# Second pass of Q and K: seven products of halves in place of four plain blocks, and the work that moves with it

## The chip, the cores and the metric

The kernel runs on one core of one Trainium2 chip. A time is device microseconds (us) of one execution. The kernel before took 1787.72 us (median of 3 executions, 1787.06 to 1787.75). The execution whose trace is read here took 1787.19 us; 1785.4 us of it is the span of the profile.

## The reference

The input x has 2048 tokens of 1024 numbers. Two branches work on it, and a gate mixes them:

```python
x = A_x
g = _sigmoid((x * gate_w).sum(-1, keepdims=True))
a = _A_ref(x, A_wqkv, A_wo)                  # 32 heads of 32; softmax(q k / sqrt(32)) v, then wo
b = _B_ref(x, B_w_q, B_k1, B_k2, B_u, B_v)   # PEER: 64 experts
return g * a + (1 - g) * b
```

In the second branch each of 32 heads multiplies x by a 1024x256 matrix `w_q`. It compares one half of the result with 8 keys `k1` and the other with 8 keys `k2`, and takes the best of each. The pair names one of 64 experts, and the output is the sum over the heads of gelu(x . u) v.

## The kernel before, in words

**Precision.** fp32 numbers are kept as a high and a low part (`split`: ACT writes the high part, DVE subtracts it to get the low one). A product of two such pairs is three matmuls per 128 rows of contraction: high by high, high by low, low by high. A 128x512 block of Q or K over the whole contraction (8 chunks of 128) is thus 24 matmuls, and a product over half the contraction is 12.

**Stages.** Q and K are made in two passes over x: tokens 1024 to 2047 first, then 0 to 1023. Each pass goes through 8 chunks of 128 output columns, for Q and K each.

- First pass: chunks 0 and 1 plain. Chunks 2 to 7 as units (`qk_unit`). A unit takes the Q and K columns of one chunk as two block rows, both halves of the contraction as two block columns, and makes the 2x2 block product with seven products of halves (`Halves`: S1 to S4 are sums of weight halves, T1 to T4 of x halves, P1 to P7 the products) in place of eight. Seven products of 12 matmuls (84) stand for four plain blocks of 24 (96).
- Second pass: all 8 chunks plain, 32 blocks of 24 matmuls (line 734).
- Router: 16 tiles of 128 tokens (`router_mm`, line 781, 24 matmuls each). DVE and POOL turn each tile into an expert number per head and side (`router_1` to `router_4`, lines 785 to 827; `router_step(t)` does the last three stages for the tiles before). The weights `Wp` of the router are `w_q` folded with the keys.
- Values: half of V plain (line 900), the rest as units (line 156). Then attention, and the output projection.

**The folds.** `w_q` times the keys is 32 `fold`s of four groups of matmuls with a 32-column stationary (line 332). Four folds share a bank; `fold_t` turns the bank round and stores the result in DRAM (WPD), from where `load_wp` fetches it and `split_wp` makes the router's weights. In the second pass a table (`between`) says after which of the 32 blocks which work is issued: nearly all folds there come in triples, behind one block.

**The evacuation.** `evac_hi` copies a result to `hi` on ACT (line 241), and `evac_lo` subtracts on DVE (line 254) and takes a largest absolute value on DVE (line 248), for a bound on the attention's scores that is compared with a limit after the router (`bound`, line 835). `store_parts` issues the two stores on ACT's DMA queue. In a unit, DVE adds the products up (line 162): P1 is copied out by ACT (line 532), then P6, P7, P5 and so on are added in SBUF.

**The gate** (z = x . gate_w) is eight multiply-adds of 128x512 on DVE for each 512 tokens (lines 663 and 665), all in the second pass; `gate_sums` adds over the partitions on PE and stores z.

**x.** The four 512-token blocks of x, in two halves each (`x_blk[n, ki]`, high and low part), stand in SBUF from the second pass to the values; those that the units have overwritten with T sums are loaded and split again in the second pass (`again`).

Each engine works through its instructions in the order in which the code issues them. In the second pass this order is set by the table; in the units by the order of the products and by the `hooks`; in the router by the loop over the tiles:

```python
for t in range(NT - 1):
    router_mm(t)
    router_step(t)
    if t >= 8 and t % 2 == 0:
        ...
        in_parts(f"B{ki + 1}{2 - ni}", ...)   # splits the V weights, 128x2048 on ACT and DVE
```

Behind the router come, on DVE, the rest of the last tiles, the experts' activation (lines 921 to 951) and, for the V units, T sums and S sums of x and weight halves with their low parts. The first V unit's products start at 509.10 us in the order P1, P2, P3, P7, ...; P1 and P2 take the weight halves in `a` (A11, A12), P3 takes the operand S4, whose low part DVE makes behind a T sum, and P7 takes S3.

## Time and profile before

| stage | us from the span's start | what PE runs |
|---|---|---|
| first chunks | 0 to 53.2 | plain blocks, tokens 1024 to 2047 |
| first pass | 53.2 to 179.8 | six units, folds 2 to 11 |
| second pass | 179.8 to 377.7 | 32 plain blocks, 20 folds |
| router | 377.7 to 465.2 | 16 tiles |
| values | 465.2 to 623 | plain, then units |
| attention | 623 to 1605 | |
| output projection | 1605 to 1785 | |

The profiled execution took 1787.19 us with a span of 1785.4 us, at a granted TensorE clock of 1.00. The median of the runs is 0.53 us above it. In the views, "busy" of PE is a modelled time of pipelined matmuls: a row of PE's timeline lasts longer than the step to the next row's start, and steps from start to start are what counts. In a DVE or ACT row, what stands in brackets is the idle time before the instruction and what ended it.

### The profile page before, as it was taken

The numbers are of one execution on the slowest core, as the hardware profiler recorded it, in microseconds if no ns is written. First come the engines' busy times: TensorE is split into PE (matmuls) and PEld (weight loads), VectorE is DVE, ScalarE is ACT, GpSimd is POOL, SyncE is SP. The second block draws the span as 40 slices with busy tenths as digits, with TensorE's granted clock in tenths as the row PEclk, the third lists the DMA queues.
The fourth block names the chain that finished last, engine by engine and source line by source line (L and its number), as shares of the span: only waits on it lengthen the run. The fifth ranks groups of instructions, "written<-read, shape, count | busy, mean of one in ns | idle before, by whom it ended". The sixth has DMA issues, their size and how long they took to land. (4 is left out here: it accounts for less than half of the span.)

```text
span 1785.4 us, 35585 instructions
## 1 busy us (share of the span) xinstructions
PE 1776.8 (100%) x14663; PEld 1006.1 (56%) x14663; DVE 1502.2 (84%) x1319; ACT 1216.6 (68%) x1613; POOL 295.8 (17%) x357
## 2 busy tenths in 40 slices
PE   9999999999999999999999999999999999999999
PEld 7777776788888843333333333333343333337887
DVE  6968776258886869999999999999999989998886
ACT  4434322221233399999999999999999999993221
POOL 0212000026501201112112121121111121221100
PEclk9999999999999999999999999999999999999999
DMA  7797888831227787779889888897898898977431
GB/s 244 240 284 246 269 276 279 280 117 72 73 100 252 272 207 164 166 162 198 186 183 210 179 194 197 179 187 169 184 205 189 182 211 191 198 160 270 140 102 72
DMA packets 138428, 343.16 MB, mean 192 GB/s; under 512 B 17452, under 2 KB 50560, under 8 KB 119940
## 3 DMA queue, kind: packets, MB, share of 16 engines
q0 software_dynamic: 24080, 139.27, 38.2%
q1 hardware_dynamic: 93876, 165.38, 28.7%
q10 hardware_dynamic: 20304, 36.18, 7.1%
q8 instruction: 116, 1.90, 0.4%
q14 instruction: 52, 0.43, 0.1%
HBM read 151.47 MB, written 86.09 MB: 133 GB/s over the span
## 5 line engine op out<-in xcount | busy, mean ns | idle before, releaser
L1154 ACT ACTIVATE P<-ring 128x512 f32<-128x512 f32 (+2 forms) x980 | 792.0, 942 | 3.2 <-PE ring L296 1.8
L1321 DVE TENSOR_TENSOR acc<-acc,P 128x2048 f32<-128x2048 f32 x199 | 455.3, 2291 | 36.9 <-ACT P L1154 23.1
L1282 PE MATMUL o<-P,V 128*32 128x512 f32 (+2 forms) x3992 | 449.3, 534 | 0.3 <-ACT P L1154 0.3
L296 PE MATMUL ring<-z,k 32*128 32x512 f32 x4224 | 345.3, 425 | 0.0
L296 PEld LDWEIGHTS ring<-z,k 32*128 32x128 f32 x4224 | 179.5, 183 | 265.0 <-ACT P L1154 200.4
L1321 DVE TENSOR_TENSOR rb<-rb,P 128x2048 f32<-128x2048 f32 x89 | 203.9, 2291 | 15.7 <-ACT P L1154 9.6
L1282 PEld LDWEIGHTS o<-P,V 128*32 128x32 f32 x3992 | 92.6, 108 | 186.3 <-issue 162.9
L296 PE MATMUL ring<-z,z 32*128 32x512 f32 x1908 | 156.5, 425 | 0.5 <-ACT P L1154 0.5
L296 PEld LDWEIGHTS ring<-z,z 32*128 32x128 f32 x1908 | 81.7, 183 | 112.8 <-ACT P L1154 76.3
L1311 POOL DMA_DIRECT2D P<-P x70 | 65.7, 939 | 374.6 <-ACT P L1154 374.6
L1154 ACT ACTIVATE wo_raw<-ring 128x512 f32<-128x512 f32 (+2 forms) x126 | 107.1, 944 | 0.0
L241 ACT ACTIVATE hi<-bk 128x512 fp32r<-128x512 f32 x40 | 23.7, 595 | 111.6 <-PE bk L734 100.0
L734 PE MATMUL bk<-xh,e 128*128 128x512 f32 x384 | 94.2, 394 | 0.0
L734 PE MATMUL bk<-xl,e 128*128 128x512 f32 x384 | 92.3, 389 | 0.0
L734 PEld LDWEIGHTS bk<-xh,e 128*128 128x128 f32 x384 | 71.0, 188 | 22.0 <-issue 3.4
L254 DVE TENSOR_TENSOR lo<-bk,hi 128x512 fp32r<-128x512 f32 x40 | 27.5, 688 | 65.2 <-ACT hi L241 65.2
L734 PEld LDWEIGHTS bk<-xl,e 128*128 128x128 f32 x384 | 72.1, 188 | 15.0
L1321 DVE TENSOR_TENSOR acc<-acc,wo_raw 128x2048 f32<-128x2048 f32 x32 | 73.3, 2292 | 4.6 <-ACT wo_raw L1154 1.4
L1154 ACT ACTIVATE vhl<-ring 128x512 f32<-128x512 f32 (+2 forms) x90 | 76.2, 923 | 0.0
L102 DVE TENSOR_TENSOR e<-wraw,e 128x512 fp32r<-128x512 f32 (+3 forms) x64 | 54.4, 857 | 25.3 <-ACT e L101 24.7
L156 PE MATMUL pa<-woh,acc 128*128 128x512 f32 x224 | 72.5, 389 | 0.0
L1329 POOL DMA_DIRECT2D acc<-acc x41 | 32.8, 800 | 229.2 <-DVE acc L1321 123.4
(304 smaller groups left out, 2484.7 us busy)
## 6 DMA issues: line engine op xcount, KB each, us to landing
P<-P POOLq DMA_DIRECT2D x70, 1024.0 KB, 10.0
wqt<-in_wq SPq DMA_DIRECT2D x26, 1024.0 KB, 6.7
wraw<-in_wqkv SPq DMA_DIRECT2D x30, 512.0 KB, 7.9
acc<-acc POOLq DMA_DIRECT2D x21, 512.0 KB, 8.4
qdh<-hi ACTq DMA_DIRECT2D x32, 256.0 KB, 5.5
qdl<-lo ACTq DMA_DIRECT2D x32, 256.0 KB, 6.0
kdh<-hi ACTq DMA_DIRECT2D x32, 256.0 KB, 2.6
kdl<-lo ACTq DMA_DIRECT2D x32, 256.0 KB, 5.7
```

The lines of the kernel that those rows point to most:

```text
L102: (on or nc.vector).tensor_tensor(out=lo, in0=src, in1=hi.bitcast(F32), op=OP.subtract)
L156: nc.tensor.matmul(ps, self.a[a][i][:, k, :], self.b[b][j][k], start=(not first and k == 0 and i == j == 0), stop=(k == HC - 1 and i == 1))
L241: nc.scalar.activation(hi, src, AF.Copy)
L254: nc.vector.tensor_tensor(out=lo, in0=src, in1=hi.bitcast(F32), op=OP.subtract)
L296: yield j, nc.tensor.matmul(ps, a[rows], b[rows], start=(i == 0), stop=(i == 2))
L734: nc.tensor.matmul(ps, t[:, kc // HC, a, kc % HC], x_at(b, n, kc), start=first, stop=last)
L1154: return nc.scalar.activation(to, ps, AF.Exp, scale=SCALE, bias=-SHIFT_LIMIT)
L1282: nc.tensor.matmul(O[h][32 * j:32 * j + 32, c0:c1], Vt[g][:, kt, 32 * j:32 * j + 32], p[:, j * 512 + c0:j * 512 + c1], start=(kt == 0), st ...
L1311: nc.gpsimd.dma_start(P[h, b], P[h, a], accum_op=OP.add)
L1321: nc.vector.tensor_add(out, a, b)
L1329: nc.gpsimd.dma_start(ACC[h][:n], ACC[h][n:2 * n], accum_op=OP.add)
```

## The change

What it does, part by part:

1. **Second pass by units.** Chunks 0 and 1 stay plain (8 blocks by `plain_block`), chunks 2 to 7 become six units. `qk_unit` serves both passes (`NB` is the first block of tokens). The T sums for it are made during the plain blocks, in places of x blocks.
2. **Three products add onto P1's bank.** In both passes P6, P7 and P4 are accumulated on P1's PSUM bank (`onto`). ACT copies the bank to SBUF after P1, after P6 and after P7; DVE adds P2 to the first copy, P5 and P3 to the second, P5 to the third. What stands in the bank after P4 is evacuated as it is. The order of the products is P1, P5, P6, P2, P7, P3, P4 (in the unit of chunk 2: P1, P2, P6, P3, P7, P5, P4).
3. **Operand copies.** The S sums move from POOL to DVE, and the copies to high and low parts follow tables (`PARTS`, `PARTS2`).
4. **Bound.** The largest absolute value on DVE becomes a sum of squares by ACT (`Square` with `accum_out`) into `junk`; the limit is squared, and what is compared is a product of two sums.
5. **Folds singly**, one between two products, in both passes (`fold_at`).
6. **The gate** is made in pieces of two multiply-adds between products, in `z`, stored in DRAM (ZPD). Parts of two token blocks (8 multiply-adds) move to the router, and `gate_sums` behind the router's tile 10.
7. **Router weights** go into the places of the units' operands; seven of the eight chunks are split in the last unit, the last one right behind it.
8. **x blocks** (1,0), (2,1), (2,0), (3,0) and (3,1) are loaded and split again during the router, at tiles 0, 2, 3, 5 and 6 (`more_x`); the first two loads (1 MB each) are issued by `load_spare` in the last unit of the second pass.

```diff
-        def product(self, name, first=None, bank=None):
+        def product(self, name, first=None, bank=None, onto=None):
             a, b = self.FACTORS[name]
-            ps = (bank or self.bank)()
+            ps = onto or (bank or self.bank)()
...
-                                     start=(not first and k == 0 and i == j == 0),
+                                     start=(not first and not onto and k == 0 and i == j == 0),
...
         nc.scalar.activation(hi, src, AF.Copy)
+        nc.scalar.activation(junk, src, AF.Square, accum_out=sq4[:, which, c, n:n + 1])
...
-        maxima.append((amax4[:, which, c, n:n + 1], hi.bitcast(F32)))
...
+        for name in order:
+            if name in ("P6", "P7", "P4"):
+                p[name] = hq.product(name, onto=p["P1"])
+            else:
+                p[name] = hq.product(name)
+            if name in ("P1", "P6", "P7"):
+                u[name] = cp.tile([128, 512], F32, name=f"u{name}")
+                nc.scalar.activation(u[name], p[name], AF.Copy)
+            made = parts.get(name, ()) if nxt else ()
+            for a in made:
+                hq.hi(a)
...
+            if name == "P1" and late:
+                evac_lo()
+            if name == "P2":
+                tt(u["P1"], u["P1"], p["P2"])
+                out(0, nb, u["P1"])
...
+            if name == "P4":
+                out(1, nb, p["P4"])
+            for a in made:
+                if a != "A11":
+                    hq.lo(a)
+                if a == "S3":
+                    hq.sums("S2")
+                    hq.sums("S4")
...
+            for f, *args in hooks.get(name, ()):
+                f(*args)
             store_parts()
...
+    ORDER = "P1", "P5", "P6", "P2", "P7", "P3", "P4"
+    PARTS = dict(P1=("A11",), P5=("S1",), P2=("A12",), P7=("S3",), P3=("S2",), P4=("S4", "A22"))
...
+    plain_block(1, 1, 1, [(hq.parts, "A22"), (hq.parts, "S1"), (combine, "T4", "xh1"), (load_w, 1, 3)])
...
+    hooks[7]["P1"] += [(wr.close,), (open_router,)]
+    hooks[7]["P6"] += [(split_wp, 0), (split_wp, 1), (split_wp, 2), (load_spare,)]
+    hooks[7]["P2"] += [(split_wp, 3)]
+    hooks[7]["P7"] += [(split_wp, 4)]
+    hooks[7]["P3"] += [(split_wp, 5), (split_wp, 6)]
+    for c in range(2, KC):
+        qk_unit(c, ORDER2 if c == 2 else ORDER, c + 1 if c < KC - 1 else None, hooks[c])
+    evac_lo()
+    store_parts()
+    nc.vector.tensor_reduce(sq, sq4, axis=AX.X, op=OP.max)
...
+    split_wp(7)
...
+    load_xr(2, 0, 0)
+    load_xr(3, 0, 1)
+    gate_load(1)
+    more_x = {0: [(from_spare, 1, 0, "xh1"), (lambda: gate(0, xr[1, 0]),)], 2: [(from_spare, 2, 1, "xl3"), (gate_store, 1)],
+              3: [(from_spare, 2, 0, "xh2"), (load_xr, 3, 1, 0), (gate_load, 3)],
+              5: [(from_spare, 3, 0, "xh3"), (lambda: gate(0, xr[3, 0]),)], 6: [(from_spare, 3, 1, "xl2")],
+              7: [(gate_store, 3), (load_zacc,)], 10: [(gate_sums,)]}
     for t in range(NT - 1):
         router_mm(t)
         router_step(t)
+        for f, *args in more_x.get(t, ()):
+            f(*args)
```

How the order of instructions moves is seen at three places. First PE in the second pass. In a row, the first name is the tile written, the names behind the arrow are the tiles read (`bk` a PSUM bank, `e` a weight operand, `xh`/`xl` a place of x, `wqt` a place of `w_q`), and the number at the end counts equal rows. Before, three folds stand in one stretch between two blocks:

```order
L734 MATMUL bk_2691<-xl_1468,e_141 128x512 x12
L332 MATMUL bk_2599<-wqt,kpad 32x512 x4
L332 MATMUL bk_2599<-wqt_1591,kpad 32x512 x4
L332 MATMUL bk_2599<-wqt_1592,kpad 32x512 x4
L734 MATMUL bk_2741<-xh_1523,e_141 128x512 x12
L734 MATMUL bk_2741<-xl_1547,e_141 128x512 x12
L353 MATMUL bk_2773<-ident,wt 128x128 x4
```

Now, in the unit of chunk 6, the products P1, P5, P6, P2, P7, P3, P4 with a fold after P5, P2 and P3; P6, P7 and P4 write the bank of P1:

```order
L167 MATMUL bk_2634<-xh_1474,e_143 128x512 x12
L167 MATMUL bk_2656<-xl_1668,e_144 128x512 x12
L338 MATMUL bk_2593<-xh_1964,kpad 32x512 x4
L167 MATMUL bk_2634<-xl_1753,e_144 128x512 x12
L167 MATMUL bk_2692<-xl_1545,e_154 128x512 x12
L338 MATMUL bk_2593<-wqt,kpad 32x512 x4
L167 MATMUL bk_2634<-xh_1706,e_143 128x512 x12
L167 MATMUL bk_2743<-xl_1569,e_154 128x512 x12
L338 MATMUL bk_2593<-xh_1964,kpad 32x512 x4
L167 MATMUL bk_2634<-xh_1924,e_154 128x512 x12
```

What moved: each fold has a product on either side, and the last product of a unit ends in a bank that started with its first. Second, DVE at the router's first tiles. Before (`router_1` of one tile, then `router_2`):

```order
L789 TENSOR_REDUCE m<-bk_3011 128x64
L790 TENSOR_SCALAR m<-m 128x64
L792 TENSOR_TENSOR eq<-bk_3011,m 128x64x7
L794 TENSOR_SCALAR eq<-m 128x64
L802 TENSOR_REDUCE mm<-eq 128x64
L804 TENSOR_TENSOR eq<-eq,mm 128x512
```

Now, with what each instruction waits for (15 more memsets of one column stand behind the first row; Activation, DVE and Pool are the engines ACT, DVE and POOL, and DMAHW0 to DMAHW7 the lanes on which the hardware DMA queues report their transfers):

```order
L767 MEMSET e_3008 128x1 [waits DMAHW4_49,DMAHW3_49]
L812 TENSOR_REDUCE m<-bk_3033 128x64 [waits DMAHW6_49,Activation_49]
L813 TENSOR_SCALAR m<-m 128x64 [waits DVE_49]
L815 TENSOR_TENSOR eq<-bk_3033,m 128x64x7 [waits DMAHW5_49,DVE_49]
L817 TENSOR_SCALAR eq<-m 128x64
L173 TENSOR_TENSOR xh_3066<-xh_2886,xh_3066 128x2048 [waits Activation_49]
L617 SCALAR_TENSOR_TENSOR junk<-xh_2886,gw,junk 128x512 [waits DMAHW6_49]
L617 SCALAR_TENSOR_TENSOR junk<-xh_2886,gw,junk 128x512 [waits DVE_49] x3
L825 TENSOR_REDUCE mm<-eq 128x64 [waits DMAHW7_49,Pool_49]
L827 TENSOR_TENSOR eq<-eq,mm 128x512 [waits DVE_49]
```

What moved: between `router_1` of tile 0 and the next tile stand the low part of an x block (128x2048) and four gate operations, and the first rows wait for transfers. Third, ACT at the end of the last unit of the second pass, now (before, ACT went from the last stores of a plain block to splitting the last two router weights, and then to `xu`):

```order
L254 ACTIVATE hi<-bk_2795 128x512 [waits DMAHW4_49,PE_49]
L255 ACTIVATE junk,sq_138<-bk_2795 128x512 [waits Activation_49]
L85 DMA qdh<-hi 128x512 [waits DMAHW1_49]
L85 DMA qdl<-lo 128x512 [waits DMAHW2_49,DVE_49]
L85 DMA kdh<-hi 128x512 [waits DMAHW3_49,Activation_49]
L85 DMA kdl<-lo 128x512 [waits DMAHW5_49,DVE_49]
L103 ACTIVATE e_154<-wpr_2884 128x448
L103 ACTIVATE e_154<-ugr 128x64
L808 ACTIVATE xu<-bk_3033 128x64 [waits DMAHW3_49,DMAHW6_49,DMAHW1_49,PE_49]
```

What moved: the split of the last router weight (into the place `e_154`) stands behind four stores, and the stores of `qdl` and `kdh` wait on lanes 2 and 3, whose transfers before these are the two 1 MB loads of `load_spare`.

## The prediction

> **What bounds the kernel now.** I read the page's busy shares first, then the busy time by stage, then the timelines of PE and DVE where stages meet, and last the groups that give prices.

> ```profile
> PE 1776.8 (100%) x14663; PEld 1006.1 (56%) x14663; DVE 1502.2 (84%) x1319; ACT 1216.6 (68%) x1613; POOL 295.8 (17%) x357
> core 0: us, PE busy (x) PEld busy (x) DVE busy (x) ACT busy (x) POOL busy (x), PEclk, DMA share, GB/s
> 53.20:179.80 126.60, 126.39 (x600) 97.62 (x597) 97.82 (x128) 47.72 (x77) 30.43 (x23) 1.00 0.82 259
> 179.80:377.70 197.90, 197.90 (x957) 149.96 (x956) 118.55 (x163) 53.72 (x77) 3.84 (x5) 1.00 0.83 264
> 382.75:429.94 47.19, 47.19 (x210) 38.80 (x209) 32.94 (x66) 3.93 (x10) 25.30 (x31) 1.00 0.26 91
> 429.94:465.00 35.06, 35.06 (x157) 29.02 (x156) 32.36 (x52) 6.87 (x9) 23.11 (x24) 1.00 0.00 0
> 465.00:514.01 49.01, 49.01 (x217) 40.28 (x216) 44.57 (x55) 15.13 (x18) 10.79 (x12) 1.00 0.22 76
> ```

> PE alone sets the time up to the values: it stands still for 0.2 us in the first pass and never after it. But the reserve behind it differs. In both passes DVE has a quarter or more of the time free. In the first half of the router it is idle for 47.19 - 32.94 = 14.25 us; from 429.94 us on it is nearly dense (32.36 of 35.06, then 44.57 of 49.01). Work that goes to DVE in the router has only those 14 us to go into. The next rows show what is waited for behind it:

> ```profile
> 500.41 1.29 DVE L102 TENSOR_TENSOR a<-xw,a 128x512 fp32r<-128x512 f32 x2
> 513.33 0.68 DVE L102 TENSOR_TENSOR xh<-xw,xh 128x512 fp32r<-128x512 f32 x1
> 516.14 1.28 DVE L102 TENSOR_TENSOR xh<-z,xh 128x512 fp32r<-128x512 f32 x2
> ...
> 509.10 2.91 PE L156 MATMUL bk<-xh,a 128*128 128x512 f32 x12
> 514.60 2.88 PE L156 MATMUL bk<-xl,xh 128*128 128x512 f32 x12
> ```

> The first V unit takes S4 at 514.60 us, which DVE has ready at 513.33 + 0.68 = 514.01: 0.59 us of reserve. Its A parts are ready at 501.70 for a product at 509.10: 7.4 us. So DVE's queue is a second path, nearly as long as PE's at 514 us, that starts with the router.

> **Part 1, fewer products.** A product of halves steps by 2.72 us, 0.2267 per matmul:

> ```profile
> 190.72 2.88 PE L734 MATMUL bk<-xh,e 128*128 128x512 f32 x12
> 193.44 2.88 PE L734 MATMUL bk<-xl,e 128*128 128x512 f32 x12
> ```

> Six units of 84 for 24 blocks of 24 matmuls take 72 away: **-16.3 us**. The first pass keeps its 84 per unit.

> **Part 2, single folds.**

> ```profile
> 198.88 2.88 PE L734 MATMUL bk<-xl,e 128*128 128x512 f32 x12
> 205.54 2.66 PE L734 MATMUL bk<-xl,e 128*128 128x512 f32 x11
> 265.01 2.88 PE L734 MATMUL bk<-xl,e 128*128 128x512 f32 x12
> 273.40 2.89 PE L734 MATMUL bk<-xl,e 128*128 128x512 f32 x12
> 306.86 1.07 PE L680 MATMUL bk<-zacc,ones 128*32 128x512 f32 x8
> 307.74 2.76 PE L332 MATMUL bk<-wqt,kpad 128*32 128x512 f32 x24
> ```

> Between 198.88 and 205.54 lie two products and one fold: 6.66 - 5.44 = 1.22 us for it. Between 265.01 and 273.40 lie two products and three folds: 8.39 - 5.44 = 2.95. A join that is cut costs (3 x 1.22 - 2.95) / 2 = 0.355. Eight triples and a pair are cut, 17 joins: **+6.0**. The sums of the gate leave this stage: **-0.9** (306.86 to 307.74). The passes lose 11.2 us.

> **Part 3, what the units ask of DVE and ACT.**

> ```profile
> L162 DVE TENSOR_TENSOR u<-u,bk 128x512 f32<-128x512 f32 x24 | 16.0, 682 | 0.3
> L102 DVE TENSOR_TENSOR e<-wraw,e 128x512 fp32r<-128x512 f32 x35 | 28.3, 815 | 11.0 <-ACT e L101 10.6
> L101 ACT ACTIVATE e<-wraw 128x512 fp32r<-128x512 f32 x34 | 20.8, 621 | 11.6 <-DVE wraw L138 5.7 <-POOL wraw L138 3.8 <-DVE lo L254 2.1
> L532 ACT ACTIVATE c<-bk 128x512 f32<-128x512 f32 x6 | 3.5, 580 | 0.0
> ...
> L665 DVE SCALAR_TENSOR_TENSOR zacc<-xh,ugr,zacc 128x512 f32<-128x512 f32 x22 | 16.5, 750 | 0.6
> L241 ACT ACTIVATE hi<-bk 128x512 fp32r<-128x512 f32 x31 | 18.5, 597 | 106.0 <-PE bk L734 96.8 <-issue 3.5 <-DVE amax L248 3.4
> L101 ACT ACTIVATE e<-wraw 128x1024 fp32r<-128x1024 f32 x15 | 15.9, 1057 | 19.1 <-DMA wraw<-in_wqkv 10.6 <-DVE zacc L665 7.4 <-ACT hi L241 1.0
> ```

> A unit with three folds takes PE 84 x 0.2267 + 3 x 1.22 = 22.7 us. DVE has four adds, four low parts of results and four S sums at 0.68, seven low parts of weights at 0.82 and some six gate operations at 0.75: 18.4 us. ACT has three copies at 0.58, four results at 0.60, seven weight parts at 0.62, and four Squares. No row has a Square that sums; I bound it by 0.597 (the same shape) and 1.057 (twice the width) and take the lower end, whose shape it has: 10.9 us, 12.7 at the upper end. Neither engine reaches PE's 22.7. P6, P7 and P4 must wait until ACT has copied P1's bank, but one whole product (2.72 us) of another bank lies before each of the three, against a copy of 0.58; the cover goes only where ACT's queue is over 2 us late. I take +0.7 over all twelve units for such meetings, between 0 and 4 (a copy's 0.58 in six of them). The sums that leave POOL, the maxima that leave DVE and the adds saved lie in DVE's and POOL's free time: nothing.

> **Part 4, the router.** DVE now also splits five x halves there and runs eight gate operations.

> ```profile
> 383.65 0.62 DVE L789 TENSOR_REDUCE m<-bk 128x64 f32<-128x448 f32 x1 [0.91 <-ACT xu L785]
> 429.94 2.78 DVE L102 TENSOR_TENSOR xh<-xh,xh 128x2048 fp32r<-128x2048 f32 x1 [0.74 <-ACT xh L101]
> 453.31 2.28 DVE L102 TENSOR_TENSOR xh<-xh,xh 128x2048 fp32r<-128x2048 f32 x1
> 455.51 0.68 DVE L827 TENSOR_REDUCE packed<-pq 128x16 f32<-128x512 f32 x1
> 460.08 0.68 DVE L827 TENSOR_REDUCE packed<-pq 128x16 f32<-128x512 f32 x1
> ...
> 377.76 0.39 PE L781 MATMUL bk<-wph,xh 128*128 128x512 f32 x1
> ```

> A low half costs 455.51 - 453.31 = 2.20, a gate operation 0.75: 5 x 2.20 + 8 x 0.75 + 0.4 for two small operations of the new bound = 17.4 us. A router step that follows such work takes 460.08 - 455.51 = 4.57. I count from PE's first router matmul (377.76). Before, the first reduction starts at 5.9 and tile 8's first stage ends at 429.20 (429.94 less the wait), that is 51.4. Now it ends at 5.9 + 1.5 (tile 0) + 8 x 4.57 + 17.4 = 61.4. DVE is 10.0 us late there; the wait of 0.74 and the slower operation (2.78 for 2.28) at 429.94 are swallowed, and 8.7 stay, since behind it DVE is dense.

> Then the start. What the first reductions wait for now are the last stores of the results: before, ACT had issued the last one by 379.81, 2.0 us after the router's first matmul. Now P3's result comes just ahead of P4's, and a high part, a Square and two stores (0.6 + 0.6 + 0.8) more stand in the queue: 4.0 us.

> ```profile
> 379.39 0.42 ACTq L83 DMA_DIRECT2D kdl<-lo  x1
> kdh<-hi ACTq DMA_DIRECT2D x32, 256.0 KB, 2.6
> kdl<-lo ACTq DMA_DIRECT2D x32, 256.0 KB, 5.7
> xl<-in_xT SPq DMA_DIRECT2D x3, 1024.0 KB, 12.6
> ```

> Landing takes 2.6 to 5.7 us, so DVE's first row is free at about 6.6 to 9.7 where it started at 5.9: +0.7 to +3.8, I take +2.2, the middle.

> S4 is then ready at 136.25 + 8.7 + 2.2 = 147.15 after the router's first matmul, and P3 took it at 136.84: **+10.3** (the 0.9 of the gate's sums, now in the router, goes into that wait). The A parts are ready at 123.94 + 10.9 = 134.8, where PE is at 132.2; so PE waits twice, 2.6 us at P1 and 147.15 - 140.3 = 6.9 us at P3. Behind the waiting P3 stands everything up to the last V unit, and behind that the attention, which ACT fills; nothing makes the loss good.

> **The clock.** The kernel has one long stretch without PE, its end:

> ```profile
> 1782.00:1783.00 1.00, 0.00 (x0) 0.00 (x0) 0.32 (x1) 0.00 (x0) 0.00 (x0) 1.00 0.12 44
> 1783.00:1784.00 1.00, 0.00 (x0) 0.00 (x0) 0.00 (x0) 0.00 (x0) 0.00 (x0) 0.87 0.63 218
> 1784.00:1785.40 1.40, 0.00 (x0) 0.00 (x0) 0.00 (x0) 0.00 (x0) 0.00 (x0) 0.50 0.00 0
> ```

> After more than 1.7 us without a matmul the granted clock is 0.50. A wait of 6.9 us should do the same, and P3 would run at half speed. How soon the clock comes back no row shows. The cost lies between 0 and 2.6 (P3 wholly at half speed is 5.44, and P7 would have waited for S3 anyway, ready 2.81 after S4 by the DVE rows at 513.33 and 516.14). I take **+2.0**, nearer the upper end, as the wait is long against 1.7. [...]

> **Sum:** -16.3 + 6.0 - 0.9 + 0.7 + 10.3 + 2.0 = +1.8 against the profiled 1787.19, thus 1789.0; the median of the runs lies 0.5 above the profiled one: **1789.5 us**.

> **Rivals.**

> *The gain arrives.* DVE makes up for most of its extra work: its waits for ACT's `xu` and for POOL vanish when it is late, and the x splits move into them more than my steps of 4.57 allow. If 3 of the 8.7 us are left and the stores land early, PE waits 3 us or less, and the clock stays: 1787.7 - 10.5 + 3 = 1780.2; with 6 left, 1783.2. For it speaks the idle 14.25 us, nearly as much as the added 17.4; against it that I have already used up 7.4 of it, and that a step seen behind other work still takes 4.57. Between: 1782.

> *The stores come late (slower).* In the last unit, `load_spare` puts two 1 MB loads on lanes that the stores of `qdl` and `kdh` must wait for. Such a load landed in 12.6 us; they are issued after the third of seven products, some 11 us before the router, and share the engines with each other. If they land at 12.6, the stores go out as I assumed; if they take twice that, 25 us, ACT's queue stands until 14 us after the router's start, with the router's last weight and `xu` behind the stores, and DVE starts some 6 us later than assumed. Beyond 2 us it decides: 1789.5 + 5 = 1794.5. For it speaks the DMA share of 0.83 in the second pass; against it that the loads of weights have ended by then.

> *The units stall.* Each unit waits 0.6 us or so at three copies for ACT: 12 x 0.6 = 7, thus 1796. Against it stands ACT's load of about half.

> *The change does not do what it says*, because the new bound sends the kernel the general way: only if the drawn inputs exceed the limit, which they do not by a wide margin (largest product of sums 12,879, worked out from the inputs, against 28,800).

> **How the numbers follow.** The forecast's own case gets 0.45, the gain 0.29, the late stores 0.20, the stalls 0.05, the last 0.01. In the likeliest case the bounds (start 0.7 to 3.8, meetings 0 to 4, clock 0 to 2.6) give 1785 to 1794. With the two neighbours the range is 1781 to 1795. About 0.2% (3.6 us) is what a measurement tells from no change, so "same" is 1784.2 to 1791.3: faster 0.30 (the gain), same 0.41 (the forecast without its upper tail), slower 0.29 (late stores, stalls, that tail).

> **What would show it.** In the profile after: the router's first matmul 10 to 11 us earlier (367) with PE dense before it; DVE's first router reduction 6.6 to 9.7 after that; DVE without waits for `xu` after tile 0; tile 8's first stage ending near 63.6 after the router's start; a PE wait of some 7 us at the first V unit's P3, with a lower clock behind it. The forecast is wrong if DVE reaches S4 less than 5 us late, if ACT's stores are issued later than 7 us into the router, or if the units lose more than 4 us.

## The result: 3% slower, most of it in the first pass

The changed kernel took 1840.66 us (median of 4, 1838.66 to 1844.44) beside 1787.39 before: a ratio of 1.0302 (95% interval 1.0282 to 1.0321). The prediction was 1789.5 with a range to 1795. The profiled execution took 1838.66 us with a span of 1836.9, 51.5 more than before. By stages, read from PE's timeline:

| stage | before | after | difference | predicted |
|---|---|---|---|---|
| up to the first unit | 53.2 | 54.3 | +1.0 | 0 |
| first pass, six units | 126.6 | 160.0 | +33.4 | +4.6 |
| second pass | 197.9 | 194.8 | -3.1 | -15.1 |
| router's first matmul to the first V unit | 131.3 | 149.7 | +18.3 | +12.3 |
| behind it | 1276.3 | 1278.1 | +1.8 | 0 |

(The two predicted figures of the passes are the prediction's sum of -10.5, split by where the folds stand: two folds more and three cut triples in the first pass, 2 x 1.22 + 6 x 0.355 = 4.6. Differences are taken before rounding.)

The page's busy row, and the stages (busy time of PE, its weight loads, DVE, ACT and POOL; then the granted clock, the share of the DMA engines and GB/s):

```profile
PE 1783.9 (97%) x14591; PEld 999.0 (54%) x14591; DVE 1524.8 (83%) x1352; ACT 1293.8 (70%) x1812; POOL 277.5 (15%) x337
54.26:214.28 160.02, 141.31 (x617) 102.91 (x614) 97.08 (x140) 70.94 (x140) 2.43 (x3) 0.93 0.77 232
214.28:409.12 194.84, 185.12 (x862) 134.76 (x861) 123.97 (x172) 92.00 (x187) 3.75 (x5) 0.99 0.79 242
422.00:470.00 48.00, 48.00 (x214) 39.39 (x213) 43.85 (x81) 13.20 (x16) 25.81 (x23) 1.00 0.41 142
501.36:558.79 57.43, 46.12 (x194) 37.68 (x193) 52.08 (x70) 12.03 (x15) 19.86 (x22) 0.88 0.19 65
```

PE, which before stood still for 0.2 us in the first pass, now stands still there for 18.7 and runs at 0.93 of its clock, while DVE, at 97 of 160 us, is no busier than it was. No engine is full: somebody waits in a queue. PE's list of waits (engine, line and what it waited for; us in total, times, longest), and PE's timeline with the five waits of the first pass:

```profile
PE bk L167 <- DVE lo L261: 20.4, 6, 6.4
PE bk L954 <- DMA zt<-zd: 11.3, 1, 11.3
PE bk L167 <- ACT uP L545: 5.7, 2, 2.9
```

```profile
62.82 4.31 PE L167 MATMUL bk<-xh,e 128*128 128x512 f32 x12 [2.82 <-ACT uP L545]
94.37 7.33 PE L167 MATMUL bk<-xl,e 128*128 128x512 f32 x24 [2.92 <-ACT uP L545]
117.38 4.27 PE L167 MATMUL bk<-xl,e 128*128 128x512 f32 x12 [1.86 <-DVE lo L261]
147.14 5.49 PE L167 MATMUL bk<-xl,e 128*128 128x512 f32 x12 [4.73 <-DVE lo L261]
179.18 5.10 PE L167 MATMUL bk<-xl,e 128*128 128x512 f32 x12 [6.38 <-DVE lo L261]
```

After each wait the product itself is longer than its 2.88 us (7.33 for 5.74 where the row holds two products): over the five rows the granted clock was 0.66, 0.77, 0.67, 0.50 and 0.56. The queues of DVE and ACT before the longest of these waits show why:

```profile
167.32 0.69 DVE L152 TENSOR_TENSOR e<-wraw,e 128x512 fp32r<-128x512 f32 x1 [2.74 <-ACT e L148]
177.11 0.69 DVE L142 TENSOR_TENSOR wraw<-wraw,wraw 128x512 f32<-128x512 f32 x1 [9.09 <-DMA wraw<-in_wqkv]
177.83 0.69 DVE L142 TENSOR_TENSOR wraw<-wraw 128x512 f32<-128x512 f32 x1
178.44 0.68 DVE L261 TENSOR_TENSOR lo<-bk,hi 128x512 fp32r<-128x512 f32 x1
...
179.16 0.34 ACTq L85 DMA_DIRECT2D kdl<-lo  x1
179.60 0.63 ACT L148 ACTIVATE e<-wraw 128x512 fp32r<-128x512 f32 x1 [12.31 <-DVE lo L261]
180.61 0.59 ACT L545 ACTIVATE uP<-bk 128x512 f32<-128x512 f32 x1
```

At the head of a unit DVE subtracts S3, which needs K's weights for the next chunk. They are still being loaded: DVE stands for 9.09 us. Behind S3 on DVE is the low part of the last unit's last result (line 261), made straight from the bank in which P4 ended, and P2 of the new unit takes that bank next; ACT's queue holds the store of the low part, and behind the store the copy of P6 that P7 needs. It starts at 180.61, though P6 had begun at 169.78 and takes 3.0 us: ACT had stood for 12.31 us. So one late transfer stops DVE, ACT and PE.

The weights were just as late before: in the units, S3 was begun 10.6 to 16.4 us after the unit's first product, and is now begun after 9.5 to 14.0 (the first products counted out in steps of 2.72 us). In the old trace it was POOL that made S3 (its waits in the first pass, and its timeline), and nothing stood behind it on POOL that made PE wait. (Of the 98.0 us, 65.7 are POOL's first wait, which began before the units.)

```profile
POOL s L138 <- DMA wraw<-in_wqkv: 98.0, 4, 65.7
```

```profile
83.57 1.29 POOL L138 TENSOR_TENSOR s<-wraw,wraw 128x512 f32<-128x512 f32 x1 [9.08 <-DMA wraw<-in_wqkv]
108.56 1.29 POOL L138 TENSOR_TENSOR s<-wraw,wraw 128x512 f32<-128x512 f32 x1 [11.60 <-DMA wraw<-in_wqkv]
133.59 1.28 POOL L138 TENSOR_TENSOR s<-wraw,wraw 128x512 f32<-128x512 f32 x1 [11.62 <-DMA wraw<-in_wqkv]
```

The timelines of PE, DVE and SP's queue at the router and the values:

```profile
409.12 0.84 PE L804 MATMUL bk<-wp,xh 128*128 128x512 f32 x3
416.75 1.38 PE L804 MATMUL bk<-e,xl 128*128 128x512 f32 x3 [2.71 <-ACT e L103]
423.22 0.06 DVE L767 MEMSET e<- 128x1 f32 x1 [5.87 <-DMA kdh<-hi]
423.58 0.62 DVE L812 TENSOR_REDUCE m<-bk 128x64 f32<-128x448 f32 x1
480.05 0.22 DVE L817 TENSOR_SCALAR eq<-m 128x64 f32<-128x64 f32 x1
...
522.02 0.31 SPq L85 DMA_DIRECT2D zt<-zd  x1
523.70 0.26 PE L954 MATMUL bk<-ident,zt 16*128 16x16 f32 x1 [11.31 <-DMA zt<-zd]
523.89 13.31 PE L937 MATMUL bk<-xl,xl 128*128 128x512 f32 x48
558.79 1.54 PE L167 MATMUL bk<-xh,a 128*128 128x512 f32 x6
```

DVE's first reduction comes 14.5 us after the router's first matmul (5.9 before), tile 8's first stage ends at 71.2 (51.4 before). The last store was issued at 415.59, 6.5 us after the router's first matmul. PE waits 11.31 us, not at P1 and P3 as predicted but earlier, at the transposition of z, and the block behind it takes 13.31 us for 11.04, at a granted clock of 0.83.

### The profile page after: what moved, and what is told of

Read it like the earlier page. It is cut to its first block, busy times and chain, and to the rows that moved or that the text cites. A ratio compares the mean times of both kernels' runs of the same rounds, so it can differ in the third digit from the quotient of the medians.

```text
span 1836.9 us, 35630 instructions
## 1 busy us (share of the span) xinstructions
PE 1783.9 (97%) x14591; PEld 999.0 (54%) x14591; DVE 1524.8 (83%) x1352; ACT 1293.8 (70%) x1812; POOL 277.5 (15%) x337
## 5 line engine op out<-in xcount | busy, mean ns | idle before, releaser
L167 PE MATMUL bk<-xl,e 128*128 128x512 f32 x504 | 131.2, 415 | 23.4 <-DVE lo L261 20.4
L167 PEld LDWEIGHTS bk<-xl,e 128*128 128x128 f32 x504 | 99.6, 201 | 55.1 <-DVE lo L261 23.0
L167 PE MATMUL bk<-xh,e 128*128 128x512 f32 x504 | 123.0, 398 | 2.8 <-ACT uP L545 2.8
L167 PEld LDWEIGHTS bk<-xh,e 128*128 128x128 f32 x504 | 93.7, 189 | 37.4 <-issue 7.5
L148 ACT ACTIVATE e<-wraw 128x512 fp32r<-128x512 f32 x70 | 42.9, 627 | 98.4 <-DVE lo L261 62.1
L152 DVE TENSOR_TENSOR e<-wraw,e 128x512 fp32r<-128x512 f32 x70 | 47.4, 687 | 41.0 <-ACT e L148 38.0
L85 POOL DMA_DIRECT2D wpd<-wt x8 | 6.2, 773 | 387.3 <-ACT wt L362 387.3
## 6 DMA issues: line engine op xcount, KB each, us to landing
P<-P POOLq DMA_DIRECT2D x70, 1024.0 KB, 10.8
wqt<-in_wq SPq DMA_DIRECT2D x17, 1024.0 KB, 8.1
xh<-in_wq SPq DMA_DIRECT2D x9, 1024.0 KB, 10.5
qdh<-hi ACTq DMA_DIRECT2D x32, 256.0 KB, 3.9
qdl<-lo ACTq DMA_DIRECT2D x32, 256.0 KB, 3.5
kdh<-hi ACTq DMA_DIRECT2D x32, 256.0 KB, 5.8
```

The source lines that it names most:

```text
L85: return queue.dma_start(a, b)
L148: nc.scalar.activation(self.a[name][0], self.raw[name], AF.Copy)
L152: nc.vector.tensor_tensor(out=lo, in0=self.raw[name], in1=hi.bitcast(F32), op=OP.subtract)
L167: nc.tensor.matmul(ps, self.a[a][i][:, k, :], self.b[b][j][k], start=(not first and not onto and k == 0 and i == j == 0), stop=(k == HC - ...
```

## The experiments

In what follows "router" is the time of the router's first matmul (377.76 before, 409.12 after, 367 by count without a wait), and "to V" is the time from there to the first V unit's first product (131.3 and 149.7). The kernel before, run beside them, took 1787 to 1790; the runs were made in batches, and totals of different batches can differ by these 2 to 3 us. Each is a single run unless a range is given. How much chance is in one trace is seen where nothing was changed: kernels with the same passes differ by up to 3.5 us in the router's start (374.81 and 378.28 below), kernels with the same router by up to 1.5 us in to V (149.5 to 151.0). Theory A is that the order of DVE's and ACT's queues makes the loss in the units, its rivals that the weights are late for any order (B) or the transfer engines full (C). Theory E is that DVE's queue from the router's start sets where the V units begin.

**The low part first.** In `qk_unit`:

```diff
+            if name == "P1" and late:
+                evac_lo()
             made = parts.get(name, ()) if nxt else ()
             for a in made:
                 hq.hi(a)
...
-            if name == "P1" and late:
-                evac_lo()
```

> One line moved in the units of both passes: the low part of the unit's last result (DVE) is issued ahead of the next operand's copies and sums, not behind them. Theory A (queue order): PE waits because that low part, and with it ACT's store and its copies, stands on DVE behind S3, which waits for K's weights. Then the waits of PE for DVE's low part (20.4 us, 6 times) go to about 0; what is left is ACT's copy of P6 behind the high part of S1, which still waits for the weights: up to 4 us per late load, some 10 us in all, with the router's first matmul at 375 to 385 us in place of 409.12. Theory B (late weights stall PE whatever stands behind them): the waits only change their name, router's start at 400 or later. In both, the wait for zt in the values stays at 11 us.

**Four buffers** for the raw weights:

```diff
-        i = w_no[0] % 3
+        i = w_no[0] % 4
...
-        nc.scalar.activation(junk, src, AF.Square, accum_out=sq4[:, which, c, n:n + 1])
+        nc.scalar.activation(lo, src, AF.Square, accum_out=sq4[:, which, c, n:n + 1])
```

> Four buffers for the raw weights in place of three (the Square writes into the low part's tile, which frees the room), order of instructions as in the change. K's weights for the next chunk but one no longer wait for the last unit's operands. Theory A and B both say that the weights' lateness goes: DVE's waits for them (26.3 and 19.6 us in the two passes) fall to below 5 us, and the router's first matmul comes at 368 to 374 us (367 is the count without any wait). If the loads are late because the transfer engines are full (theory C), the waits stay above 15 us in each pass and the router's start above 395.

Both edits together:

> Both edits. Theory A: no wait in the units is left, router's start at 367 to 371 us, little better than four buffers alone; theory C: like the low part first alone. The router and the values are untouched: DVE's first reduction some 14 us after the router's start, the wait for zt about 11 us, total about 1800 us.

| | total | router | PE's waits in the units |
|---|---|---|---|
| low part first | 1818.38 | 388.02 | copies on ACT 9.2 us, fold turn 3.1 |
| four buffers | 1814.93 | 384.45 | one for the low part 6.2, copies 4.8 |
| both | 1813.68 | 383.28 | copies 4.7, fold turn 3.6 |

Each edit alone brings the router 21 and 25 us forward, both 26. Low part first leaves the weights as late as they were (DVE still waits 21.9 and 25.4 us for them in the two passes) and still regains 21.1: it is the order, as theory A says. Theory B falls with that, and theory C with the second edit, which cuts DVE's waits for weights to 9.7 and 2.5 us. But the forecasts were too good (375 to 385, found 388; 368 to 374, found 384), and with both edits 16 us above the count are left where at most 4 were expected.

**The sums on POOL again**, the changed kernel otherwise:

```diff
-                    hq.sums("S3")
-                    hq.sums("S1")
+                    hq.sums("S3", nc.gpsimd)
+                    hq.sums("S1", nc.gpsimd)
```

> The changed kernel with one part of the change undone: the sums S3 and S1, which wait for K's weights at the head of a unit, are made on POOL again, not on DVE; the order of everything else and the three buffers stay. Theory A (DVE's queue held by the weights): DVE no longer waits for weights (26.3 and 19.6 us before), the low part of the last result goes out in time, and the waits of PE for it (20.4 us) vanish; the high part of S1 on ACT still waits, so the units keep some waits for ACT's copy of P6; router's first matmul at 380 to 392 us in place of 409.12. Theory B (the weights come too late for any order): 400 or later.

Router at 400.38, total 1830.91: 8.7 us regained, less than theory A said, and just past the line that was drawn for theory B (400 or later). The waits for the low part are gone, but

```profile
PE bk L167 <- ACT uP L545: 16.4, 7, 3.8
ACT e L148 <- POOL wraw L142: 42.3, 4, 12.1
```

(PE's waits, and ACT's in the first pass): now ACT's queue is held: the high part of S1 waits for POOL's sum, and behind it stands the copy of P6, for which P7 waits since it adds onto the same bank. That is the second half of the theory, and the next run takes it alone.

**S1 behind the copy of P6** (three buffers, low part first):

```diff
-    PARTS = dict(P1=("A11",), P5=("S1",), P2=("A12",), P7=("S3",), P3=("S2",), P4=("S4", "A22"))
+    PARTS = dict(P1=("A11",), P6=("S1",), P2=("A12",), P7=("S3",), P3=("S2",), P4=("S4", "A22"))
```

> Three buffers, low part first as in that run (router's first matmul 388.0 us there), and one thing more: ACT makes the high part of S1, which waits for K's weights, behind its copy of P6, not ahead of it (S1 moves from P5 to P6 in the table of operands). Theory A, second half (what the weights' lateness still cost after the first edit went through ACT's queue): PE's waits for ACT's copies (9.2 us, 5 times) fall to about 4 (the unit of chunk 2 keeps its 2.8), the wait for the turn of the folds (3.1) goes, router at 378 to 382. If the weights themselves are too late by now, it stays at 386 or more.

PE's waits in this kernel:

```profile
PE bk L954 <- DMA zt<-zd: 9.3, 1, 9.3
PE bk L167 <- ACT uP L545: 6.3, 4, 2.6
PE bk L804 <- ACT e L103: 4.6, 1, 4.6
```

Router at 373.93, better than forecast, total 1805.16; the fold's turn is no longer waited for. Two changes of order, with the weights little earlier than they were (DVE still waits 23.3 and 18.8 us for them, 26.3 and 19.6 in the changed kernel), move the router by 35.2 us: the passes are now 3.8 us faster than in the kernel before.

**The folds in triples again** (on both first edits): all three folds of a unit at P3.

```diff
-        fold_at(n, 3 + i // 3, ("P5", "P2", "P3")[i % 3], n + 3 if n < 9 else None,
+        fold_at(n, 3 + i // 3, "P3", n + 3 if n < 9 else None,
```

(and likewise in the second pass.)

> On top of low part first and four buffers: seven groups of three single folds (2 to 10 in the first pass, 20 to 31 but for two in the second) stand together behind P3 again. By the price of the prediction (1.22 a single fold, 2.95 a triple) the router's first matmul comes 7 x 0.71 = 5.0 us earlier, at 378.3 in place of 383.3. If single folds cost nothing more here, or if PE then waits for copies whose cover the folds were, it stays at 382 to 385.

The router comes at 392.40, 9.1 us later (total 1822.82), not 5.0 earlier. The single fold's price is what the prediction said: from 382.92 to 392.31 us in the changed kernel lie three products and one fold, 9.39 - 3 x 2.72 = 1.23. But what the folds do for the queues is worth more: PE's waits for ACT's copies grow from 4.7 us (2 times) to 12.3 (9 times), for the fold's turn from 3.6 to 7.5, and DVE's wait for weights from 9.6 to 17.0 in the first pass and from 3.8 to 11.6 in the second. A single fold lies between two products as cover, and its 1 MB load is issued alone. Which of the two counts more was not separated.

**The router's loads.** First the two loads of the last unit are issued behind the last stores:

```diff
-    hooks[7]["P6"] += [(split_wp, 0), (split_wp, 1), (split_wp, 2), (load_spare,)]
+    hooks[7]["P6"] += [(split_wp, 0), (split_wp, 1), (split_wp, 2)]
...
     evac_lo()
     store_parts()
+    load_spare()
```

> The two 1 MB loads of x for the router are issued behind the last stores of Q and K, not in the middle of the last unit. Theory D (the stores wait behind these loads): ACT issues the last store about 3 us after the router's first matmul in place of 6.5, DVE's first reduction comes 7 to 9 us after it in place of 14.5, PE's wait for the router's last weight (2.71) goes, and the wait for zt falls from 11.3 to about 5, unless the x blocks that now land later hold DVE up at tiles 0 and 2. Total 6 to 9 us less than 1838.7. Rival: the first rows of DVE wait for landings that take as long without the loads; then the start stays above 12 us. The units are untouched (router's start at 409).

Total 1843.39. DVE's first reduction comes 15.2 us after the router's first matmul (428.83 after 413.60), not 7 to 9. But the edit did not do what it was meant to do. The queues of SP and ACT, in the changed kernel (first row) and in this one:

```profile
402.03 0.97 SPq L85 DMA_DIRECT2D xh<-in_xT  x2
406.51 0.97 SPq L85 DMA_DIRECT2D xh<-in_xT  x2
420.90 0.34 ACTq L85 DMA_DIRECT2D kdh<-hi  x1
421.77 0.58 ACT L103 ACTIVATE e<-wpr 128x448 fp32r<-128x448 f32 x1 [3.40 <-DMA xh<-in_xT]
```

SP issues the two loads 7.1 us before the router's first matmul in both kernels: moving the lines of code does not hold SP back, whose queue comes to these loads behind the fetches of the router's weights either way. And the store of `kdh` goes out 7.3 us into the router, behind a stand of ACT that the profile puts down to one of these loads. So theory D, by which the stores wait for the lanes of these two loads, was not tested, and stays open. Next the other two loads of the router's start go to ACT's queue behind tile 0 (on both unit edits):

```diff
-    load_xr(2, 0, 0)
-    load_xr(3, 0, 1)
...
-    more_x = {0: [(from_spare, 1, 0, "xh1"), ...
+    more_x = {0: [(load_xr, 2, 0, 0, nc.scalar), (load_xr, 3, 0, 1, nc.scalar), (from_spare, 1, 0, "xh1"), ...
```

> On top of both edits of the units (low part first, four buffers): the two 1 MB loads of x that the router's start issues go to ACT's queue behind tile 0's work, so that only the two loads of the last unit and the stores are under way at the router's start. Theory D2 (the last stores land late because 4 MB of loads share the engines with them, not because of the lane order): DVE's first reduction comes 8 to 11 us after the router's first matmul in place of 14.9, PE's wait for the last router weight shrinks from 3.6 to below 2, and the wait for zt from 9.4 to about 5; first V product 143 to 146 us after the router's first matmul in place of 149.5. Rival (the order of ACT's queue alone: buffers and lanes): nothing changes, the start stays at 14 us or more. If the later x blocks become the limit, DVE waits at tiles 3 and 5.

The first reduction comes at 10.5 us (394.25 after 383.77) for 14.9, DVE's wait for the store of `kdh` shrinks from 5.45 to 1.65, and to V is 146.1 for 149.5; PE's waits shrink less than forecast (the last router weight 3.6 to 2.9, zt 9.4 to 7.3). The total is 1809.19 for 1813.68, but the kernel before, too, was 2.1 us faster beside this run. ACT issues the last store hardly earlier (6.6 us into the router, 7.1 without the edit); the stores land earlier. So some 4.4 of the 8.6 us that DVE starts late come from these two loads standing where they did. That they slow the stores by sharing the transfer engines is the author's guess (in the changed kernel the DMA share was 1.06 from 409.30 to 416.00 us), but it is not shown alone: the 256 KB load of z, which had stood behind them on SP's queue, goes out with the edit at 377.70 in place of 390.05.

**DVE's work in the router** (each on both unit edits, to V 149.5 there; the times from the router's first matmul decide, since the totals come from two batches). Without the gate:

```diff
-(from_spare, 1, 0, "xh1"), (lambda: gate(0, xr[1, 0]),)]
+(from_spare, 1, 0, "xh1")]
```

(the same at tile 5)

> On top of the same two edits, the eight gate operations in the router are left out (the gate's sums of these tokens are then incomplete); the loads and stores around them stay. Theory E (DVE's queue through the router sets the end of the wait for zt, one for one): 8 x 0.75 to 0.9 = 6 to 7 us of DVE work go, the wait for zt falls from 9.4 to about 3, the first V product comes 143 us after the router's first matmul in place of 149.5. Rival F (zt waits for the chain of gate stores, loads and sums): the wait falls only if that chain shortens, by 2 us or less.

Without the low parts of the remade x:

```diff
     def from_spare(n, ki, place):
-        again(n, ki, place, xr[n, ki])
+        again_hi(n, ki, place, xr[n, ki])
+        no_low.add((n, ki))
```

> On top of the same two edits, the low parts of the five x blocks that are remade in the router are left out (the matmuls read the high part in their place). Theory E: 5 x 2.2 to 2.5 = 11 to 12 us of DVE work go, more than the wait for zt, which vanishes; the first V product comes about 140 us after the router's first matmul, and the clock stays at 1.00 in the values. Rival F: the wait for zt stays near 9.

And a place for zt that does not wait for the router's end:

```diff
-    zt = sm2.tile([NT, 128], F32, name="zt")
+    zt = sm.tile([NT, 128], F32, name="zt")     # beside packed, ahead of the router
```

> On top of the same two edits, the tile zt gets a place of its own in the router's first pool, so that its load need not wait until the router's last tiles leave theirs. Theory E (DVE is late as a whole): PE no longer waits at zt, but at the first V unit's products instead, for the A parts at P1 or S4 at P3, together 6 to 10 us; the total changes by less than 3 us. Rival G (only zt's place makes the loss): the wait goes and comes back nowhere, total 9 to 11 us less than 1813.7.

| | total | to V | PE waits in the values for |
|---|---|---|---|
| both unit edits | 1813.68 | 149.5 | zt 9.4 us |
| without gate | 1807.93 | 143.9 | zt 3.4 |
| without low parts | 1801.82 | 139.3 | S4's parts at P3 0.9 |
| zt early | 1813.01 | 149.4 | the gate's bank 6.8, P3 0.7 |

Theory E holds: taking 6 to 7 us of DVE work away takes 5.6 us off, taking 12 away takes 10.2 off and the wait for zt with it. Giving zt a place moves the wait to the next thing that hangs on DVE, not to P1 or P3 as forecast, and leaves to V as it was: PE waits for ACT's copy of the gate, and ACT's row ahead of it had stood 26.5 us until a T sum of DVE's was done. Where PE waits is chance; that DVE is late is the cause.

**Repairs together.** Five more kernels combine them. The first has both unit edits, triples, the loads on ACT's queue, and T4's parts behind the copy of P1 in the unit of chunk 2:

```diff
-             [..., (hq.parts, "S1"), (combine, "T4", "xh3"), (folds, (1,), (2,))]]
+             [..., (hq.parts, "S1"), (folds, (1,), (2,))]]
...
-    hooks[2]["P1"] += [(to_spare, "xl3"), (load_wq, 3), (load_wq, 4)]
+    hooks[2]["P1"] += [(combine, "T4", "xh3"), (to_spare, "xl3"), (load_wq, 3), (load_wq, 4)]
```

(and likewise in the second pass.)

> Low part first, four buffers, folds in triples, the router's first x loads behind ACT's queue, and T4's parts behind the copy of P1 in the unit of chunk 2 (its wait of 3.0 us at P6 and the slow clock behind it go). By the sum of the parts: 1813.7 - 5 (folds) - 4.5 (loads, as measured) - 4 (T4) = 1800; DVE's lateness in the router (17 us of low parts and gate operations) stays, so it does not beat the kernel before (about 1788).

1818.2 us (median of 4, 1815.1 to 1821.3; ratio 1.0172, 1.0155 to 1.0189), 18 more than forecast. The router comes at 391.60, as late as with the triples alone (392.40), and PE's waits for copies (11.2 us) and for the fold's turn (6.7) are like those of the triples. With single folds, S1 at P6 (the edit above) and T4 moved in the first pass alone:

> Low part first, four buffers, S1 at P6, T4's parts behind the copy of P1 in the first pass, the router's first x loads on ACT's queue, single folds. Both queues repaired and the weights early: no wait in the units but small ones, the count without waits is 367; router's first matmul at 370 to 375, the router and values as with the loads on ACT's queue alone (first V product 146 us later), total 1795 to 1801.

1800.93 us, router at 374.81, to V 146.7: the fastest of the runs with the change, and at the upper end of what was forecast. Then the experts' activation in pieces, behind P1, P2, P3, P7 and P4 of the first V unit and P7, P5, P6 and P2 of the second:

```diff
-    peer_counts()
...
-    Ahl = peer_act(ng)
...
+            for f in PEER.get((u, k), ()):
+                f()
```

> As the one before, and the experts' activation (about 13 us on DVE that stood ahead of the first V unit's operands) is cut into pieces that are issued within the first two V units. Theory E (DVE's queue from the router to the first V unit is the second path): what PE waits for at the first V unit then comes from DVE 13 us earlier; the wait for zt (7 us) stays, since it hangs on the router's last tile, so the total gains less than 3 us and may lose where the pieces stand ahead of the next unit's operands.

1813.64: to V is 145.6, which is no difference beside the scatter, but PE then waits 8.65 us for the activation at its transposes behind the second V unit. Another 3.5 us are the router's start (378.28), ahead of which nothing was changed. Then the gate out of the router as well, made from the raw x in a plain block of each pass:

```diff
+              (folds, (0,), (1,)), (lambda: gate(0, raws[0][:, :, 512:], True),), (gate_store, 3)],
...
+                          (lambda: gate(0, raw_of(1, 0), True),)])
```

> As the one before, and the gate of the two token blocks is made in the two passes from the raw x (4 and 8 operations; the router has none). Theory E: 6 to 7 us of DVE work leave the router and the wait for zt goes; first V product 139 to 141 us after the router's first matmul; total 7 us less than the one before, about 1790, unless DVE in the passes has no room for the 12 operations (9 us in 100 us with 80% load).

1808.69 (median of 4; ratio 1.0123, 1.0106 to 1.0140), 5 less than the one before, not 7, and not about 1790: to V falls to 136.2 and the wait for zt to 0.9, as theory E says; the other wait, 8.66, stays. (In this kernel the gate reads places of x that the sums T had overwritten already, so its z holds other sums than the reference's; the amount of work is the same.) The last two, without and with the activation in pieces, make the gate before the T sums (four operations ahead of the first pass's units, eight at the end of its last unit), and split the last router weight ahead of the last stores:

```diff
+    gate(0, raws[0][:, :, 512:], True)
+    gate_store(3)
     for name, place in (("T1", "xh0"), ("T3", "xl1")):
...
-    hooks[7]["P4"] += [(lambda: again_lo(1, 1, raw_of(1, 1)),)]
+    hooks[7]["P4"] += [(lambda: again_lo(1, 1, raw_of(1, 1)),), (lambda: gate(0, raw_of(1, 0), True),),
+                       (lambda: gate(1, raw_of(1, 1)),), (gate_store, 1)]
...
+    split_wp(7)
     evac_lo()
     store_parts()
...
-    split_wp(7)
```

> All repairs of the units (low part first, four buffers, S1 at P6, T4 behind the copy of P1), the router's first x loads on ACT's queue, no gate operation in the router (they are made in the passes from the raw x before the T sums overwrite it), and the last router weight split ahead of the last stores. Theory E: the router starts at 373 to 379 us, PE does not wait for the last router weight, the wait for zt is below 1 us, the first V product comes 135 to 138 us after the router's first matmul (131.3 in the kernel before), total 1787 to 1794: level with the kernel before or a little slower, since the five low parts stay in the router.

> The same, with the experts' activation cut into pieces within the first two V units and its transposes one unit later (after the third). If DVE's queue up to S4 is still what PE waits for, the first V unit starts or runs 2 to 4 us earlier than in the one before; if that wait is gone already, the pieces only load the V units, and the total is the same or up to 4 us worse.

1804.47 (median of 4; 1.0092, 1.0075 to 1.0108) and 1807.53 (median of 4; 1.0112, 1.0095 to 1.0129), where 1787 to 1794 was forecast. To V is 139.0 and 135.8, so the router is near the kernel before, but it starts at 385.5, not at 373 to 379: the passes had no room for the gate at those places. Waits in PE's timeline of the first of the two, and below them SP's queue there:

```profile
44.51 3.29 PE L535 MATMUL bk<-xh,e 128*128 128x512 f32 x12 [1.78 <-ACT e L103]
169.25 12.80 PE L167 MATMUL bk<-xh,e 128*128 128x512 f32 x48 [2.54 <-ACT uP L566]
215.15 1.94 PE L337 MATMUL bk<-wqt,kpad 128*32 128x512 f32 x8 [3.46 <-DMA wqt<-in_wq]
278.52 4.50 PE L167 MATMUL bk<-xl,e 128*128 128x512 f32 x12 [2.60 <-ACT uP L566]
...
186.20 22.50 SPq L85 DMA_DIRECT2D zpd<-z  x2
208.80 0.37 SPq L85 DMA_DIRECT2D wqt<-in_wq  x1
```

The longest of them is the same mistake in a third queue. The store of the eight new gate operations holds SP's queue for 11.0 us until DVE has done them, and the load of `wqt` behind it goes out at 208.80, where it went out at 197.47 in the kernel of 1800.93 us.

No version beat the kernel before. What stays open is whether the gate can be placed in the passes without these waits.

## Why the prediction was wrong, step by step

- **Part 1 and 2, counts: right.** A product steps by 2.72 us and a single fold costs 1.23. But the 6.0 us called a loss was no loss that could be undone: triples cost 9.1 more.
- **Part 3, what the units ask of DVE and ACT, is the step that failed.** It said that the sums which leave POOL "lie in DVE's and POOL's free time: nothing". Their working time does; their waiting does not. POOL waited 9 to 12 us for the weights in each of three units of the old trace, and the change moved that wait, with the sums, into the queue of an engine that others wait for. The prediction counted busy time (18.4 and 10.9 of 22.7 us) and took that for room (in the first pass DVE's free time was 23%, a little less than the quarter that it read). It is only half of it, though: with the sums back on POOL 8.7 us came back, since the new order of products also makes PE wait for ACT's copies, and ACT's copy of P6 stood behind the high part of S1. The same part named the condition rightly ("the cover goes only where ACT's queue is over 2 us late") and gave it 0.7 us; ACT stood for up to 12.31. The low part first and S1 at P6 regain 35 of the 42 us by which the passes were missed.
- **The rival "the units stall"** had the right place and, at a chance of 0.05 and 7 us, neither the size nor the cause.
- **Part 4, DVE in the router: right in size.** From its first reduction to tile 8's first stage DVE took 45.5 us before and 56.7 now, +11.1 for a predicted +10.0. Five low parts were 12.6 us for 11.0 (the first 3.42), eight gate operations 7.3 for 6.0.
- **The start: too small.** +8.6 us for 2.2, beyond the bound of 3.8. The last store was issued at 6.5 us, not 4.0, and DVE's first row came 8.3 us after the store of `kdh` that it waited for, where the medians were 2.6 to 5.7. The rival of the late stores came true in amount (DVE some 6 us later than assumed). Half of it went when the two loads of the router's start were moved; whether the lane order, the rival's reason, made the rest was not tested.
- **Where PE waits: wrong, with no effect.** Predicted 2.6 us at P1 and 6.9 at P3, found 11.3 at zt, whose place the router's last tile frees; to V is set by DVE in either case.
- **The clock: right in size (2.0, found 13.31 - 11.04 = 2.3 at zt)**, but it was counted once; behind six waits in the units the product was slower too, some 11 us together (4.31, 4.27, 5.49, 5.10 and, at 324.13, 4.38 for 2.88; 7.33 for 5.74; the granted clock over these six rows was 0.50 to 0.77). That the clock stays at waits of 3 us or less, as the rival "the gain arrives" has it, was shown by no row and did not hold: behind waits of 1.86, 2.82 and 2.92 us it fell to 0.50, behind 2.07, 2.40 and 2.71 us it stayed at 1.00. How soon it came back here, which no row had shown, is in the last section.
- Of the Square's two bounds: 0.6 us and 0.19 for reading the sum out, between the ends; what it costs was not tested by itself.

## What to carry to other kernels

When an operation moves from one engine to another, move its waits with it: look up in the old trace not what the operation costs but how long its engine stood before it, and then read what is queued behind it in the new place. An engine that is 17% busy, as POOL was, may be the one that takes the late transfer for all others (here in waits of 9 to 12 us). And a product that adds onto a bank that must be copied first can turn a late copy into a wait of PE (16.4 us in 7 waits with the sums on POOL), so nothing that depends on a transfer may stand ahead of the copy in that queue.

## What the hardware showed that was not expected

In the changed kernel the granted clock fell after a wait of 1.86 us and not after some longer ones. The wait of 1.86 us at 117.38 was followed by a product of 4.27 us for 2.88, at a granted clock of 0.67 over that row, while it stayed at 1.00 behind the waits of 2.07 and 2.40 us of these two rows of PE's timeline in the second pass:

```profile
296.81 0.66 PE L359 MATMUL bk<-ident,wt 128*128 128x128 f32 x4 [2.07 <-DVE lo L261]
376.07 3.06 PE L167 MATMUL bk<-xl,e 128*128 128x512 f32 x12 [2.40 <-DVE lo L261]
```

```profile
115.44:118.86 3.42, 1.56 (x7) 1.24 (x7) 2.25 (x4) 1.06 (x2) 0.00 (x0) 1.00 1.05 426
118.86:122.27 3.41, 3.41 (x11) 1.87 (x13) 3.34 (x6) 0.69 (x2) 0.00 (x0) 0.50 0.41 157
292.94:296.35 3.41, 1.80 (x8) 1.13 (x7) 1.58 (x3) 0.00 (x0) 0.00 (x0) 1.00 1.03 301
296.35:299.76 3.41, 2.95 (x15) 2.53 (x16) 2.24 (x4) 1.55 (x3) 0.69 (x1) 1.00 1.03 426
412.41:415.82 3.41, 1.63 (x8) 1.01 (x6) 0.99 (x4) 1.17 (x3) 0.00 (x0) 1.00 1.06 311
```

The wait of 1.86 us lay within one stretch. PE was busy for 1.56 us of it, and the clock fell at its end, 1.5 us after PE had gone on. The waits of 2.07 and 2.40 us were cut in two by the end of a stretch: PE was busy for 1.80 us or more on either side, and the clock stayed at 1.00. It stayed there after 1.63 us too, in the stretch with most of the wait of 2.71 us at the router's start. Between 2.81 and 617.21 us of this trace a stretch at a clock of 1.00 was followed by one at 0.50 each of the seven times that PE was busy for 1.56 us of it or less, and never when PE was busy for 1.63 us or more. A stretch at 0.50 was followed by one at 1.00 where PE was busy for 2.94 us of it or more; after one with 2.44 us, or less, the clock was still 0.50. That is one trace, and nothing here shows why. In the passes a fall lasted one or two stretches, and most of the time lost was in the first product: 1.4 us there for the wait of 1.86 us, 2.6 for 4.73 (5.49 - 2.88), 2.2 for 6.38 (5.10 - 2.88).
